# Boot in written order on VectorE and ScalarE, level 16 and u of block 1 moved to ScalarE, loads hung behind levels and updates

## The chip, the cores and the metric

The kernel runs on one core of a Trainium2 chip. The metric is the device time of one execution in microseconds (us). Profiles are of single executions; the span that a profile shows is about 1.7 us shorter than the time of the same run.

## The reference

A linear attention with per-step decay (4 batches, 8 heads, 768 tokens, head size 48), whose output, laid out as 3072 tokens by 384, goes through a dense layer:

```python
for t in range(S):
    cur = np.einsum('bhd,bhe->bhde', u[None] * kt, vt)
    y[:, :, t] = np.einsum('bhd,bhde->bhe', rt, state + cur)
    state = wt[:, :, :, None] * state + np.einsum('bhd,bhe->bhde', kt, vt)
x = y.transpose(0, 2, 1, 3).reshape(B * S, H * D)      # 3072 x 384
h = x @ w_in                                           # 384 x 2048
g = h - np.tanh(h)
return g @ w_out                                       # 2048 x 384
```

## The kernel before

The 3072 tokens are eight blocks of 384 (four batches, two halves each). For each block the attention is made in *levels*: at level m (1, 2, 4, 8, 16, 32) TensorE makes the scores between the two halves of every stretch of 2m tokens, the part that is wanted is copied into `scores`, and VectorE multiplies `kq` and `rp` by the decays of that stretch. Then come *turn* (k transposed, copied to `ks` by ScalarE), *update* (`states`, by VectorE) and *result* (two groups of matmuls, whose copies make `xT`).

```python
def level(self, ps, m, p0, n):
    if m == L // 2:                       # 32: a layout without a mask
        self.last_level(ps, p0, n)        # its copies are ScalarE's
        return self.decay(m, p0, n)
    gr = self.gram(ps, self.tiles["kq"], self.tiles["rp"], p0, n, m, L // 2)
    ins = self.decay(m, p0, n)
    ...
    for h in range(2):
        ...
        nc.vector.copy_predicated(out=dst, mask=mask, data=src)
    return ins
```

The dense layer of block i runs in 16 steps f, and the attention of block i+1 is laid between the steps. A step is: six matmuls `hp`, six results on ScalarE (`h`, `s`, `qa`, `qb`, `th`, `big`), five products on VectorE (`rest`, from `hs` to `gT`), and, three steps later, six matmuls `acc`.

Weights arrive as 64-bit words in 16 chunks of 768 KB, one for each step. Each is *converted* on the chip by two operations of ScalarE and three of VectorE:

```python
def convert(f, raw, _):
    ...
    nc.scalar.activation(out=a.bitcast(F32), in_=hi.bitcast(F32), func=AF.Copy, scale=HIGH_SCALE)
    nc.scalar.activation(out=up, in_=lo.bitcast(U32), func=AF.Copy, scale=2.0 ** -29)
    return [
        lambda: nc.vector.tensor_single_scalar(a, a, 3, op=ALU.logical_shift_left),
        lambda: nc.vector.scalar_tensor_tensor(out=a, in0=hi, scalar=-2 ** 31, in1=a,
                                               op0=ALU.bitwise_and, op1=ALU.bitwise_or),
        lambda: nc.vector.tensor_tensor(out=a, in0=a, in1=up, op=ALU.add)]
```

*Boot* is what comes before the first `hp`: the whole attention of block 0, and chunks 0 to 5. There TensorE and SyncE ran in written order, and a scheduler placed the instructions of VectorE and ScalarE. The other ten chunks are converted inside the first block, at the steps listed in `converted`:

```python
steps = (1, 2, 3, 4, 5, 6, 8, 10, 12)       # of level 1, 2, 4, 8, 16, 32, turn, update, result
before = {0: ("kmix", "rmix", "totals 1", "totals 2", "kq")}
behind = {1: ["rp"]}
converted = (0, 3, 4, 5, 5, 8, 9, 10, 11, 11)
```

`kmix` and `rmix` multiply half of k and r by u on VectorE. Last, in boot, six moves of 24 KB (`fill_holes`, `xT<-late`) copy rows that the result's layout can't put in place. The first `hp` needs them.

## Time and profile before

| | before |
|---|---|
| median, range of 4 runs | 679.27 us, 678.1 to 680.3 |
| span of the profile | 678.6 us |
| busy: TensorE, VectorE, ScalarE | 643.7, 567.3, 470.2 us |
| first `hp` begins | 49.47 us |
| VectorE begins the states of block 1 | 113.00 us |
| block 1 begins | 135.02 us |

The last rows are starts in the timeline. They cut the run into boot, the first block and the rest.

### The profile page before, as it was taken

The numbers are of one execution on the slowest core, as the hardware profiler recorded it, in microseconds if no ns is written. First come the engines' busy times: TensorE is split into PE (matmuls) and PEld (weight loads), VectorE is DVE, ScalarE is ACT, GpSimd is POOL, SyncE is SP. The second block draws the span as 40 slices with busy tenths as digits, with TensorE's granted clock in tenths as the row PEclk, the third lists the DMA queues.
The fourth block names the chain that finished last, engine by engine and source line by source line (L and its number), as shares of the span: only waits on it lengthen the run. The fifth ranks groups of instructions, "written<-read, shape, count | busy, mean of one in ns | idle before, by whom it ended". The sixth has DMA issues, their size and how long they took to land.

```text
span 678.6 us, 19964 instructions
## 1 busy us (share of the span) xinstructions
PE 643.7 (95%) x8480; PEld 412.9 (61%) x8480; DVE 567.3 (84%) x1139; ACT 470.2 (69%) x920; POOL 9.8 (1%) x30
## 2 busy tenths in 40 slices
PE   3847999999999999999999999999999999999997
PEld 3734656656665666656665666656666566655554
DVE  7899999999986998689984999769986899756764
ACT  4346779985677757686576856777576865768785
POOL 2010000000000000000000000000000000000000
PEclk9968989999999999999999999999999999999999
DMA  8788141204012321025012140124110200001000
GB/s 312 219 286 319 67 140 47 92 36 142 2 50 90 98 80 50 10 82 176 3 48 92 36 141 3 48 90 142 38 48 15 98 17 2 1 11 36 0 0 36
DMA packets 30840, 54.36 MB, mean 80 GB/s; under 512 B 2336, under 2 KB 28704, under 8 KB 30752
## 3 DMA queue, kind: packets, MB, share of 16 engines
q1 hardware_dynamic: 28960, 44.20, 19.6%
q0 software_dynamic: 1584, 8.65, 3.6%
q8 instruction: 67, 1.10, 0.7%
q10 hardware_dynamic: 208, 0.25, 0.1%
q14 instruction: 21, 0.17, 0.1%
HBM read 47.19 MB, written 4.72 MB: 76 GB/s over the span
## 4 chain that ended last, share of the span: by engine, by line
PE 78%; DVE 7%; issue 4%; PEld 4%; DMA 3%; ACT 3%; PEldq 0%; SPq 0%; DVEq 0%; ACTq 0%
PE acc L524 33%; PE hp L486 31%; PE att L238 9%; DVE states L349 2%; PE att L386 2%; PEld hp L486 2%; PE att L321 2%; PEld att L368 1%; DMA raw<-in_weights 1%; PE att L302 1%; DMA xT<-late 1%; PEld acc L524 1%; DMA wt<-in_wT 1%; DVE kq L270 1%; DVE hs L503 1%
## 5 line engine op out<-in xcount | busy, mean ns | idle before, releaser
L486 PE MATMUL hp<-xT,w_sb 128*128 128x384 f32 x768 | 273.4, 493 | 8.4 <-DMA xT<-late 6.8
L524 PE MATMUL acc<-w_sb,gT 128*128 128x384 f32 x768 | 275.0, 495 | 0.0
L486 PEld LDWEIGHTS hp<-xT,w_sb 128*128 128x128 f32 x768 | 147.6, 193 | 112.5 <-ACT up L169 7.0
L524 PEld LDWEIGHTS acc<-w_sb,gT 128*128 128x128 f32 x768 | 140.7, 190 | 89.2 <-ACT o L529 2.3
L493 ACT ACTIVATE h<-hp 128x384 f32<-128x384 f32 x128 | 62.7, 490 | 163.0 <-PE hp L486 162.4
L508 DVE TENSOR_TENSOR th<-h,th 128x384 f32<-128x384 f32 x128 | 70.9, 554 | 43.2 <-ACT th L497 43.1
L503 DVE SCALAR_TENSOR_TENSOR hs<-h,s 128x384 f32<-128x384 f32 x128 | 71.0, 555 | 23.2 <-ACT s L494 23.0
L511 DVE COPY_PREDICATED gT<-big,th 128x384 f32<-128x384 int32 x128 | 76.1, 595 | 12.8 <-ACT th L497 0.5
L495 ACT ACTIVATE qa<-s,shift 128x384 f32<-128x384 f32 x128 | 78.8, 615 | 4.2
L503 DVE SCALAR_TENSOR_TENSOR gT<-qb,hs 128x384 f32<-128x384 f32 x128 | 71.4, 558 | 9.7 <-PE hp L486 0.5
L498 ACT ACTIVATE big<-s,shift 128x384 f32<-128x384 f32 x128 | 76.8, 600 | 0.0
L496 ACT ACTIVATE qb<-s,shift 128x384 f32<-128x384 f32 x128 | 76.7, 599 | 0.0
L503 DVE SCALAR_TENSOR_TENSOR hs<-qa,hs 128x384 f32<-128x384 f32 x128 | 70.6, 551 | 0.0
L494 ACT ACTIVATE s<-h 128x384 f32<-128x384 f32 x128 | 67.0, 524 | 4.1
L238 PEld LDWEIGHTS att<-rp,kq 48*64 48x64 f32 x3072 | 54.7, 148 | 22.5 <-issue 18.9
L497 ACT ACTIVATE th<-h 128x384 f32<-128x384 f32 x128 | 64.9, 507 | 0.0
L238 PE MATMUL att<-rp,kq 48*64 48x32 f32 x3072 | 58.4, 231 | 6.1 <-issue 6.0
L270 DVE TENSOR_TENSOR kq<-kq,tot 128x768 f32<-128x768 f32 (+1 forms) x45 | 38.7, 859 | 2.6 <-PE att L238 2.6
L285 DVE COPY_PREDICATED scores<-mask_all,att 128x384 f32<-128x384 uint8 (+1 forms) x72 | 40.3, 621 | 0.0
L270 DVE TENSOR_TENSOR rp<-rp,tot 128x768 f32<-128x768 f32 (+1 forms) x45 | 38.8, 863 | 0.0
L349 DVE SCALAR_TENSOR_TENSOR states<-states,tot,att 128x48 f32<-128x48 f32 x176 | 31.5, 256 | 6.7 <-PE att L339 6.7
L238 PE MATMUL att<-rmix,kmix 48*64 48x64 f32 x768 | 14.5, 232 | 8.8 <-ACT rmix L219 6.1
(50 smaller groups left out, 338.8 us busy)
## 6 DMA issues: line engine op xcount, KB each, us to landing
raw<-in_weights POOLq DMA_DIRECT2D x11, 768.0 KB, 6.7
rmix<-in_rT SPq DMA_DIRECT2D x7, 768.0 KB, 4.7
kmix<-in_kT SPq DMA_DIRECT2D x7, 768.0 KB, 6.5
wt<-in_wT SPq DMA_DIRECT2D x7, 768.0 KB, 7.3
kq<-in_kT SPq DMA_DIRECT2D x7, 768.0 KB, 4.4
rp<-in_rT SPq DMA_DIRECT2D x7, 768.0 KB, 4.8
v_sb<-in_v SPq DMA_DIRECT2D x8, 576.0 KB, 5.7
out_y<-o SPq DMA_DIRECT2D x23, 192.0 KB, 2.0
```

Of the source, the lines that this page charges most:

```text
L238: nc.tensor.matmul(dst, lhsT=lhs[rows, t0:t0 + L], rhs=src, start=True, stop=True)
L270: ins = nc.vector.tensor_tensor(out=part, in0=part, in1=by, op=ALU.mult)
L486: nc.tensor.matmul(hp, lhsT=w_in_sb[:, f, kc, :], rhs=xT[:, kc, :], start=(kc == 0), stop=(kc == KC - 1))
L494: nc.scalar.activation(out=s, in_=h, func=AF.Square)
L495: nc.scalar.activation(out=qa, in_=s, func=AF.Square, bias=shift[:, 0:1])
L496: nc.scalar.activation(out=qb, in_=s, func=AF.Square, bias=shift[:, 1:2])
L497: nc.scalar.activation(out=th, in_=h, func=AF.Tanh)
L498: nc.scalar.activation(out=big, in_=s, func=AF.Relu, bias=shift[:, 2:3])
L503: return lambda: nc.vector.scalar_tensor_tensor(out=out, in0=in0, scalar=scalar, in1=in1, op0=op0, op1=ALU.mult)
L508: lambda: nc.vector.tensor_tensor(out=th, in0=h, in1=th, op=ALU.subtract),
L511: lambda: nc.vector.copy_predicated(out=g, mask=big.bitcast(I32), data=th)]
L524: nc.tensor.matmul(acc, lhsT=g[:, j * P:(j + 1) * P], rhs=w_out_sb[:, f, :], start=(f == 0), stop=(f == NF - 1))
```

## The change

The intent: bring the first `hp` forward, take work off VectorE where it is the full engine (boot and the first block), and remove TensorE's gaps there. The diff at its core, much shortened:

```diff
 # level 16 is copied by ScalarE, without a mask
+            if 2 * m % 32 == 0:
+                for par in range(2):
+                    for b in range(nb):
+                        ...
+                        nc.scalar.copy(out=dst[:, :, :, t0:t0 + m], in_=src[:, :, :, b, :])
+                return ins
 # the plan of the first block
-            steps = (1, 2, 3, 4, 5, 6, 8, 10, 12)
-            before = {0: ("kmix", "rmix", "totals 1", "totals 2", "kq")}
+            steps = (1, 2, 3, 4, 5, 7, 9, 10, 12)
+            before = {0: ("totals 1", "totals 2", "kq")}
-            converted = (0, 3, 4, 5, 5, 8, 9, 10, 11, 11)
+            converted = (0, 3, 4, 4, 6, 9, 9, 10, 11, 11)
 # written order in boot on all four engines
-    ctx.enter_context(tc.manual_schedule(engines={PE, SP}))
+    ctx.enter_context(tc.manual_schedule(engines={PE, SP, DVE, ACT}))
+    def boot(ps, blk, later):
 ...                                   # first half's totals early, between the two mixes
+        for m in (2, 4, 8, 16, 32):
+            for p0 in HALVES:
+                ins = blk.level(ps, m, p0, UP)
+                ...
+            begin_behind(ins, background.pop(0)())      # a load begins behind each level
+            if m <= 8:
+                ready.append(convert(*raws.pop(0)))     # ScalarE's part of chunks 0, 1, 2
+            if m in (8, 16):                            # u of block 1, by ScalarE
+                later.mix(0, NPAIR, ("rmix" if m == 8 else "kmix",), copies=False)
+        converted()                                     # VectorE's part of chunk 0
+        for p0 in HALVES:
+            blk.turn(ps, p0)
+        converted()                                     # chunk 1
+        for _ in range(2):
+            ready.append(convert(*raws.pop(0)))
+        begin_behind(blk.update(ps, h1), later.load("kq", kT, 0, NPAIR))
+        begin_behind(blk.update(ps, h2), more_weights(nc.sync))         # load of chunk 5
+        blk.result(ps, [h1, h1 + 1])
+        blk.fill_holes([nc.sync, nc.scalar, nc.sync, nc.scalar, nc.sync, nc.sync])
+        blk.result(ps, [h2, h2 + 1], True)
+        converted()                                     # chunk 2
+        more_weights(nc.sync)
+        later.load("rp", rT, 0, NPAIR)
+        more_weights(nc.sync)
+        later.load_v()
+        ready.append(convert(*raws.pop(0)))             # ScalarE's part of chunk 5
+        while ready:
+            converted()                                 # chunks 3, 4, 5
+            if ready:
+                more_weights(nc.gpsimd)
```

## The prediction

> **What bounds the kernel now.** The page first: the share of the span that each engine is busy says TensorE (95%), but that is an average over two regimes, so I went to the forty slices and then to the stretches that they suggest.
>
> ```profile
> PE   3847999999999999999999999999999999999997
> DVE  7899999999986998689984999769986899756764
> PEclk9968989999999999999999999999999999999999
> ```
>
> From the fifth slice on TensorE is full. Before that it isn't, while VectorE is, and the clock granted to TensorE dips in slices 3, 4 and 6. The same by stage: boot up to the first transposes, end of boot, the first matmuls of the first dense block, its middle, its end, and one whole later block:
>
> ```profile
> 0.00:32.00 32.00, 18.92 (x587) 17.86 (x588) 25.44 (x67) 13.19 (x25) 3.87 (x19) 1.00 0.77 264
> 32.00:49.50 17.50, 8.04 (x292) 6.66 (x290) 15.88 (x40) 8.81 (x14) 2.80 (x5) 0.72 0.87 277
> 49.50:70.50 21.00, 16.89 (x224) 10.03 (x224) 20.02 (x33) 10.57 (x20) 1.05 (x2) 0.75 0.83 300
> 70.50:97.50 27.00, 25.41 (x439) 16.20 (x440) 26.69 (x44) 22.07 (x40) 2.11 (x4) 0.94 0.27 90
> 97.50:135.00 37.50, 37.36 (x381) 23.62 (x380) 36.57 (x80) 34.87 (x65) 0.00 (x0) 1.00 0.24 79
> 135.00:213.30 78.30, 78.16 (x1070) 49.81 (x1069) 67.75 (x138) 54.73 (x110) 0.00 (x0) 1.00 0.20 65
> ```
>
> The columns after the stretch's length are busy us of PE, PEld, DVE, ACT and POOL, then granted clock, DMA share, GB/s. In the last row, which stands for 543 us of the 678.6, TensorE works 78.16 of 78.30 us: nothing that relieves VectorE or ScalarE there can show. In rows 1 to 5 VectorE is the full one (20.02 of 21.00, 26.69 of 27.00, 36.57 of 37.50). So the change can win only before 135 us, and only as much as it shortens what VectorE does there, or what holds the end of boot.
>
> That end is read in the timeline, ScalarE, SyncE and TensorE:
>
> ```profile
> 38.45 0.48 ACT L399 COPY xT<-att 128x384 f32<-128x384 f32 x1 [1.47 <-PE att L386]
> 41.25 0.92 ACT L168 ACTIVATE w_sb<-raw 128x768 f32<-128x768 f32 x1 [2.32 <-DMA raw<-in_weights]
> 42.06 0.47 ACT L399 COPY late<-att 128x384 f32<-128x384 f32 x1
> 42.56 2.49 SPq L406 DMA_DIRECT2D xT<-late  x4
> 44.11 0.90 ACT L169 ACTIVATE up<-raw 128x768 int32<-128x768 uint32 x1 [1.57 <-DVE w_sb L172]
> 44.91 1.91 ACT L399 COPY xT<-att 48x384 f32<-48x384 f32 x4
> 49.47 4.04 PE L486 MATMUL hp<-xT,w_sb 128*128 128x384 f32 x6 [6.84 <-DMA xT<-late]
> ```
>
> ScalarE stands 2.32 us before a weight chunk that has not landed, with the `late` copy ready behind it. The six small moves that fill the holes of xT leave only at 42.56 and the first dense matmul waits 6.84 us for them, where a later block has them in 1.9 us (median of the page's list of issues): three 768 KB loads are in flight beside them. The six matmuls take 4.04 us instead of 1.94, as the clock is at half.
>
> And inside the first dense block, VectorE then TensorE:
>
> ```profile
> 62.53 0.94 DVE L270 TENSOR_TENSOR rp<-rp,wt 128x768 f32<-128x768 f32 x1
> 63.58 2.79 PE L238 MATMUL att<-rp,kq 48*64 48x32 f32 x96 [2.58 <-issue]
> 88.93 1.01 PE L302 MATMUL att<-rp,kq 48*32 48x32 f32 x96 [1.55 <-DVE rp L270]
> ```
>
> The gap of 2.58 is labelled "issue", but it ends as rp is decayed (62.53 + 0.94): it too is VectorE. From the timeline's starts of hp, the first block takes 49.47 to 135.0, 85.5 us; a later one takes 78.24, and the first lacks the three acc groups carried over (3 x 1.94 = 5.8), so 72.4 would be free of loss. About 13 us are lost there, plus what boot itself could give.
>
> **What the Trainium skill says.** "TensorE: Matmul & The Clock Gate", section "HAM oscillation — how this bites in real kernels": idle of more than about 3.4 us sends the array back to half clock, and warming takes about as long. The trace agrees in kind: groups of six cost 4.04 and 4.17 us after the gaps of 6.84 and 2.58 and 1.94 otherwise; but here 2.58 sufficed. "Runtime: NRT & Kernel Launch", section "Instruction fetch mechanics": instructions come in blocks of 256 and the crossing is mostly hidden. Here TensorE stops 1.78, 1.09 and 0.50 us in boot, each after about 127 matmuls with their loads; the change alters none of that stream, so I leave these stops in. "DMA: Bandwidth & Descriptors", section "Queues, rings and completion order": engines go round the queues by packets and each ring is in order. That fits holes that land 6 us late behind bulk loads. "ScalarE: Activation LUTs", section "What ACT_TABLE_LOAD costs", gives a fixed part near 186 ns plus 0.833 ns an element; for 192 elements that estimates 346, and the trace has 310 for the copies of level 32, which I use.
>
> **The change, part by part.**
> Level 16 without a mask, boot. VectorE loses four copies in two pairs of 0.62 and 0.63: 1.25 us. The first pair lies before a wait for TensorE's level-16 matmuls (until 27.46), so decays end only about 0.55 earlier, 30.5 instead of 31.06; the rest turns to idle there. ScalarE gains 8 copies of 16 x 192, as level 32's (8 in 2.57): 2.6 us.
> u of block 1. VectorE loses two of 0.95, stride 0.87: 1.75. ScalarE gains 8 of 467 ns, stride 0.42: 3.4 us.
> ScalarE's new 6.0 us mostly lie in an idle 7.77 us (20.37 to 28.14). rmix lands at 16.16 + 4.6 = 20.8: its four are done by 22.5. Level 16 follows its matmuls: 25.3 to 26.6 and 27.5 to 28.8. kmix is there by 25.2 but stands behind: 28.8 to 30.5. Level 32 then takes 30.5 to 33.0 (before: 28.14 to 30.7), and the ks copies 33.0 to 34.6 (before: from 31.27, the second from 32.55). So the state update begins at about 35.0 instead of 33.55.
> Written order on VectorE. Two whole weight chunks (0.55 + 0.95 + 0.95, stride 2.2 each) now stand before the update: 30.5 + 4.4 = 34.9. This fills the wait for ks, so VectorE does not stand idle; before, only 1.5 chunks' first parts stood there. The update ends at 39.3 (before 37.84).
> Written order on ScalarE. No weight load stands ahead of `late`. TensorE is 1.45 later than before at that place: L386 of the first half ends about 40.2, `late` at 40.0 to 40.6, holes leave at 40.6 instead of 42.56. Loads: one chunk (begun behind the update, 39.4) is the main thing in flight, and lands by 44; holes landed by about 45.5. TensorE's second half ends near 44.4 (before 42.63), the four xT copies near 46.3 (1.91 long, no weight conversion ahead). First dense matmul: 46.5 instead of 49.47, limited by the copies, not the holes: 3.0 gained. It will still run at half clock.
> VectorE from there to the states of block 1, which before begin at 113.07. From 35.0 the old work takes 113.07 - 33.55 = 79.5 us; less what now stands before the update (2.6), less u (1.75), less level 16 in step 5 (0.94 by stride), less old waits (0.57, 0.44, 0.32, 0.25: 1.6); plus a new wait of about 1.5, as chunk 5 is converted by ScalarE only after the xT copies (46.3 + 0.9, VectorE ready at 45.9), plus 0.5 for small ones. Sum: 35.0 + 79.5 - 2.6 - 1.75 - 0.94 - 1.6 + 2.0 = 109.6, so 3.5 earlier. TensorE reached the result matmuls about 1 us after the states were ready; that slack can go too. Level 32 two steps after level 16 removes the gap of 1.55 and its half-clocked matmuls (3.35 and 2.69 instead of 1.94 each, 2.2 together), but TensorE then comes upon VectorE at w_in of step 11 (two chunks converted in step 9 now) and at the states. So 3.5 to 4.5, about 4.2, at the end of the first block.
> Later blocks: two masks of 0.52 on VectorE become four copies of about 0.47 on ScalarE (28 copies, 13 us over the run), off the path: in step 8 ScalarE has 3.1 + 1.9 = 5.0 us against TensorE's 5.6.
> Sum: 680.0 - 4.2 = 675.8.
>
> **The rivals.**
> A: ScalarE becomes the bound in boot, and the first matmul gains nothing (it moves by the 1.5 us of ks, and copies wait for chunk 5). For: my ScalarE schedule is full from 27.5 to 34.6. Against: 2.32 + 1.57 us of waits for weights go. Total then about 678.5.
> B: the removed gaps and cold stretches all come back as gain (the whole 13 us, plus 3 of boot): 664 to 668. For: levels are moved for it. Against: VectorE is 95 to 99% busy from 49.5 to 97.5 and loses only 4 us of work.
> C: loads now bunch behind the holes (two chunks, rp, v and two more from GpSimd, some 5 MB at about 300 GB/s, 17 us from 43), and rp or chunk 6 is late for steps 0 and 1. It would cost 1 to 2 us: 677 to 678. The rp decay is due near 60, so I think it holds.
> D: ScalarE's extra copies delay h in each later block: 0.5 us times 6, 678 to 679. Against: it waits 162 us for hp in the run.
>
> **Range and chances.** The mechanism gives 3.5 to 4.5; clock windows and instruction fetches may shift by a gap of about 2 us either way, rivals A, C, D take away up to 3, a part of B could add 3. Median 675.8, 672.2 to 678.6 for 8 in 10. Two per cent is 13.6 us: only B entire would reach it. Faster 0.03, same 0.96, slower 0.01.
>
> **What would show it.** The first hp matmul at 46.5 (45.5 to 47.5) and not waiting for `xT<-late`; holes leaving near 40.6 and landing in under 5 us; the ks copies from 33.0 and the states from 35.0; half clock still at the first hp; a gap of 2 to 3 us still before the level-2 matmuls of step 2 and none before level 32 in step 7; states of block 1 beginning at 109 to 110; the first block ending near 130.8; later blocks of 78.2. It is wrong if ks begins before 32 (ScalarE is faster than I think: the gain could be 6), if the holes are still awaited, or if later blocks change length at all.

## More of the kernel before

All runs told of here are in the fast state. A run of one core has no second die to compare with, so its state is judged by its time alone.

## The result, and the profile after

| | runs | median us | range us | ratio of fast runs, 95% |
|---|---|---|---|---|
| before | 4 | 679.27 | 678.1 to 680.3 | |
| after | 4 | 676.65 | 676.54 to 677.44 | 0.9964 (0.9944 to 0.9985) |

A ratio is the mean time of a kernel's fast runs over that of the fast runs of the kernel before in the same rounds, so it isn't quite the ratio of the medians. The change saves 2.6 us, 0.4%. That is less than the two per cent from which a kernel counts as faster. The prediction had 4.2, counted from 680.0: the kernel before was profiled in a run of 680.4 us, above the median, and the two profiled spans differ by 2.9.

The forty slices of the changed kernel, TensorE and the clock granted to it:

```profile
PE   3767999999999999999999999999999999999997
PEclk9988999999999999999999999999999999999999
```

Against before, the dip of the clock in the sixth slice (half clock from 90.78 to 94.19 us before) is gone and those of the third and fourth remain. By stage, in the columns that the prediction explains, from the second stretch on:

```profile
32.00:49.50 17.50, 10.82 (x297) 8.63 (x296) 16.63 (x40) 10.99 (x20) 1.21 (x2) 0.87 0.71 249
49.50:70.50 21.00, 16.14 (x310) 10.16 (x309) 20.16 (x34) 12.12 (x24) 1.05 (x2) 0.79 0.87 338
70.50:97.50 27.00, 26.76 (x357) 16.73 (x357) 26.69 (x44) 25.68 (x49) 2.11 (x4) 1.00 0.26 92
...
132.50:210.50 78.00, 77.72 (x1068) 49.61 (x1067) 67.45 (x137) 55.96 (x114) 0.00 (x0) 1.00 0.19 62
```

VectorE is as full as before (20.16 of 21.00, 26.69 of 27.00), ScalarE has taken on 3.6 us between 70.5 and 97.5 (25.68, before 22.07), and the whole later block is TensorE's as before.

The end of boot in the timeline of the changed kernel (start, duration, engine, line, operation; in brackets the idle time before it and its releaser):

```profile
31.40 0.56 DVE L170 TENSOR_SCALAR w_sb<-w_sb 128x768 int32<-128x768 int32 x1
31.99 0.96 DVE L171 SCALAR_TENSOR_TENSOR w_sb<-raw,w_sb 128x768 int32<-128x768 int32 x1
33.09 0.96 DVE L173 CUSTOM_DVE_ANT_0 w_sb<-w_sb,up 128x1536 uint16<-128x1536 uint16 x1
33.97 0.55 DVE L170 TENSOR_SCALAR w_sb<-w_sb 128x768 int32<-128x768 int32 x1
...
36.52 4.28 DVE L360 SCALAR_TENSOR_TENSOR states<-states,tot,att 128x48 f32<-128x48 f32 x24
...
40.87 0.33 SPq L159 DMA_DIRECT2D raw<-in_weights  x1
41.29 2.51 SPq L418 DMA_DIRECT2D xT<-late  x4
42.71 1.93 ACT L411 COPY xT<-att 48x384 f32<-48x384 f32 x4 [2.05 <-PE att L398]
46.92 4.18 PE L466 MATMUL hp<-xT,w_sb 128*128 128x384 f32 x6 [4.25 <-DMA xT<-late]
```

Two things are to be seen. A chunk takes VectorE 2.57 us now (31.40 to 33.97). In the kernel before, where the scheduler had alternated two chunks, it took 2.20, over the same three durations:

```profile
39.50 0.55 DVE L171 TENSOR_SCALAR w_sb<-w_sb 128x768 int32<-128x768 int32 x1
39.97 0.95 DVE L174 CUSTOM_DVE_ANT_0 w_sb<-w_sb,up 128x1536 uint16<-128x1536 uint16 x1
40.84 0.95 DVE L172 SCALAR_TENSOR_TENSOR w_sb<-raw,w_sb 128x768 int32<-128x768 int32 x1
41.70 0.55 DVE L171 TENSOR_SCALAR w_sb<-w_sb 128x768 int32<-128x768 int32 x1
```

There each operation starts 0.08 us before the recorded end of the one ahead (39.50 + 0.55 = 40.05, next at 39.97). In written order the second starts 0.03 after the end of the first (31.96, 31.99) and the third 0.14 after that of the second (32.95, 33.09), because each reads what the one just ahead wrote: 0.11 and 0.22 us lost, six chunks in boot.

The other is the first `hp`: it is at 46.92, 2.55 earlier, and still waits for the holes. SyncE issues four of them from 41.29, behind the load of chunk 5 at 40.87.

The first block, TensorE and VectorE:

```profile
61.92 2.79 PE L240 MATMUL att<-rp,kq 48*64 48x32 f32 x96 [3.34 <-issue]
...
89.83 1.01 PE L313 MATMUL att<-rp,kq 48*32 48x32 f32 x96 [0.24 <-DVE rp L272]
...
107.64 0.94 DVE L173 CUSTOM_DVE_ANT_0 w_sb<-w_sb,up 128x1536 uint16<-128x1536 uint16 x1
108.73 2.17 PE L466 MATMUL hp<-xT,w_sb 128*128 128x384 f32 x6 [1.10 <-ACT qb L476]
111.06 3.58 DVE L360 SCALAR_TENSOR_TENSOR states<-states,tot,att 128x48 f32<-128x48 f32 x20
```

The gap before level 2 stands (3.34, before 2.58), the one before level 32 is gone (0.24, before 1.55), and a new one of 1.10 has come before `hp` of step 11: it is put down to ScalarE's `qb`, but ends as VectorE finishes that step's weights (107.64 + 0.94 = 108.58). The states of block 1 begin at 111.06, 1.94 earlier. Between 30 and 115 us the record has one single wait of VectorE for another engine (us in total, times, longest), where the kernel before has five, of 2.2 us together:

```profile
DVE kq L272 <- PE att L240: 0.3, 1, 0.3
```

Block 1 begins at 132.08, 2.94 earlier. From there to the end both kernels take 543.6 us.

### The profile page after: what moved, and what is told of

Its sections match the earlier page's. It is cut to its first block, busy times and chain, and to the rows that moved or that the text cites. A ratio compares the mean times of both kernels' runs of the same rounds, so it can differ in the third digit from the quotient of the medians.

```text
span 675.7 us, 19997 instructions
## 1 busy us (share of the span) xinstructions
PE 642.5 (95%) x8480; PEld 413.0 (61%) x8480; DVE 559.9 (83%) x1119; ACT 488.1 (72%) x964; POOL 7.8 (1%) x25
## 4 chain that ended last, share of the span: by engine, by line
PE 76%; DVE 11%; issue 5%; PEld 4%; ACT 2%; DMA 2%; PEldq 0%; SPq 0%; DVEq 0%; ACTq 0%
PE acc L504 32%; PE hp L466 30%; PE att L240 9%; DVE states L360 3%; PE att L398 2%; PEld hp L466 2%; PEld att L380 1%; PE att L332 1%; DVE w_sb L171 1%; DVE hs L483 1%; DVE w_sb L173 1%; PEld acc L504 1%; DVE rp L272 1%; PE att L313 1%; DMA wt<-in_wT 1%
## 5 line engine op out<-in xcount | busy, mean ns | idle before, releaser
L491 DVE COPY_PREDICATED gT<-big,th 128x384 f32<-128x384 int32 x128 | 76.2, 595 | 12.8 <-DVE gT L483 0.5
L296 DVE COPY_PREDICATED scores<-mask_all,att 128x384 f32<-128x384 uint8 (+1 forms) x54 | 32.0, 659 | 0.0
```

What stands on the lines that cost most here:

```text
L491: lambda: nc.vector.copy_predicated(out=g, mask=big.bitcast(I32), data=th)]
```

## The experiments

Three theories of what sets the gain. **V**: VectorE's queue, from boot to the states of block 1, sets the end of the first block, and every microsecond put on it or taken off it counts. **H**: the first `hp`, with the holes and the copies of xT, sets it. **G**: TensorE's gaps and half-clocked stretches in the first block set it. Beside these the prediction's rival **C**: loads that come late.

All kernels gave correct results and were timed in five rounds against the kernel before. The changed kernel itself ran as a control. Six runs each (five for the written order alone), against 10 to 12 of the kernel before, whose median was 679.32, 679.14 and 680.01 us in the three groups of kernels that ran together (first four, next four, last four). All twelve ran on one chip. Starts in their profiles, in us:

| kernel | block 0: states begin | first `hp` | block 1: totals begin | block 1: states begin | end | end less states |
|---|---|---|---|---|---|---|
| before | 33.55 | 49.47 | 52.13 | 113.00 | 678.6 | 565.6 |
| after | 36.52 | 46.92 | 51.06 | 111.06 | 675.7 | 564.7 |
| control | 36.07 | 46.64 | 50.61 | 110.61 | 675.5 | 564.9 |
| chunks alternating | 36.31 | 47.59 | 51.53 | 111.17 | 676.4 | 565.2 |
| rp decayed in step 0 | 35.58 | 46.51 | 50.12 | 111.94 | 676.5 | 564.6 |
| chunk 5 by GpSimd | 36.03 | 45.47 | 50.46 | 110.09 | 674.5 | 564.4 |
| needless VectorE work | 35.91 | 46.73 | 50.45 | 114.69 | 679.8 | 565.1 |
| u on VectorE | 36.13 | 46.73 | 52.40 | 112.41 | 677.2 | 564.8 |
| mask for level 16 | 36.37 | 47.44 | 50.91 | 111.74 | 677.2 | 565.5 |
| old plan | 36.04 | 47.17 | 50.57 | 110.61 | 675.7 | 565.1 |
| written order alone | 35.03 | 48.20 | 62.65 | 122.90 | 687.5 | 564.6 |
| chunk 5 behind the totals | 35.63 | 47.26 | 46.80 | 112.33 | 677.7 | 565.4 |
| the same, steps alternating | 35.59 | 47.38 | 46.77 | 112.02 | 677.2 | 565.2 |
| totals by GpSimd too | 36.65 | 47.64 | | 112.39 | 677.6 | 565.2 |

("Totals" are the first work of block 1 that VectorE does in the changed kernel.) The last column says most: whatever a kernel does, its span is the start of block 1's states plus 564.4 to 565.6 us, over a range of 12.8 us of that start. So what has to be explained is when VectorE begins them.

### Control, and chunks alternating in boot

Labels `e0_after` (the changed kernel, unedited) and `e1_pairs`.

> The changed kernel itself, as the control of this group. All theories: 2 to 3.5 us below the kernel before (ratio 0.995 to 0.997), first hp matmul near 46.9, states of block 1 from 111, first block ending near 132.

Measured: 676.68 us (676.26 to 677.62), ratio 0.9959 (0.9938 to 0.9980). The result stands.

```diff
-        converted()                          # three operations of one chunk in a row
-        ...
+        (s0, o0, a0), (s1, o1, a1) = ready.pop(0), ready.pop(0)
+        ...                                  # shift, and/or, add of two chunks in turn
+        for op in (s0, s1, o0, o1, a0, a1):
+            op()
+        ...
+        for op in (s2, o2, s3, a2, o3, s4, a3): ...      # and (o4, s5, a4), (o5, a5)
```

> The six weight chunks of boot converted on VectorE with the steps of two chunks alternating, so that no step stands directly behind the one it reads. Theory V (VectorE's queue up to the states of block 1 sets the end of the first block): a chunk takes 2.2 us instead of 2.57, states of block 1 begin 1.3 to 2.0 us earlier than in the changed kernel (near 109.5), total 1.2 to 2 us below it. Rival G (gaps and half clock of TensorE are what costs): the gap before level 2 in step 2 and its clock stay, total within 0.5 us of the changed kernel. Rival H (the holes of xT, that is the first hp matmul, set the total): gain only as far as the first hp comes earlier, 0.3 to 0.7 us.

Measured: 678.50 us (677.08 to 680.13), ratio 0.9986 (0.9962 to 1.0010). Chunks did come every 2.2 us, but the time was lost again. TensorE, then VectorE, of this kernel:

```profile
44.75 0.55 PE L398 MATMUL att<-scores,v_sb 64*48 64x64 f32 x22 [2.17 <-issue]
```

```profile
48.22 0.56 DVE L170 TENSOR_SCALAR w_sb<-w_sb 128x768 int32<-128x768 int32 x1 [1.75 <-ACT w_sb L167]
```

VectorE waits 1.75 us for ScalarE's part of chunk 5, which stands behind the copies of xT, and those are late (done at 47.27, in the control 45.87) because TensorE stopped 2.17 us before its last 22 matmuls of boot. The late copies explain about half of the wait: in the control ScalarE finished that part of chunk 5 at 47.26, so VectorE, ready here at 46.47, would still have waited 0.8 (an estimate from the two traces). The stop goes with a fetch of instructions: the queue that brings TensorE's began one, of 16 KB, at 42.39 in this run and at 39.49 in the control. Twelve of the fourteen profiles have a stop at this place, of 0.1 to 2.7 us, and in each TensorE goes on 2.2 to 2.5 us after this fetch begins. In the other two (control, mask for level 16) it comes there 3.5 and 4.5 us after, and doesn't stop. What sets the start of the fetch, no run shows. So V was too simple: the wait that I had predicted for the change appears only as VectorE gets faster.

### rp of block 1 decayed in step 0

```diff
-            before = {0: ("totals 1", "totals 2", "kq")}
-            behind = {1: ["rp"]}
+            before = {0: ("totals 1", "kq", "rp"), 1: ("totals 2",)}
+            behind = {}
```

> rp of block 1 decayed in step 0 right behind kq, ahead of the first activation products; the totals from 4 up come a step later. Same VectorE work. Theory V: the gap of 3.3 us before level 2 in step 2 goes, but TensorE then waits before level 4 or later by about as much; states of block 1 within 0.5 us of 111, total within 0.7 us of the changed kernel. Rival G: total 3 to 6 us lower (3.3 us of gap and some 3 us of half clock behind it). Rival H: no change.

Measured: 678.71 us (677.90 to 684.84, five of six up to 678.84), ratio 1.0003 (0.9967 to 1.0038). VectorE and TensorE:

```profile
54.76 0.96 DVE L272 TENSOR_TENSOR rp<-rp,wt 128x768 f32<-128x768 f32 x1 [2.23 <-DMA rp<-in_rT]
```

```profile
62.27 2.63 PE L240 MATMUL att<-rp,kq 48*64 48x32 f32 x96 [2.96 <-DVE scores L247]
```

It is 2.0 us over the control, more than any theory expected. rp had not landed (2.23 us of waiting, the only wait on VectorE's record here), so rival C is real where rp is wanted before about 55 us; in the changed kernel it is used at 60.88. And the gap before level 2 stayed, released now by the masks of level 1, whose PSUM buffer it takes. The gap was not removed, so this run doesn't test G.

### The load of chunk 5 by GpSimd's queue

```diff
-        begin_behind(blk.update(ps, h2), more_weights(nc.sync))
+        begin_behind(blk.update(ps, h2), more_weights(nc.gpsimd))
```

> The load of weight chunk 5, behind the state update in boot, issued by GpSimd instead of SyncE, so that the four holes that SyncE moves don't stand behind it. Holes then leave at about 40.4 instead of 41.3 on SyncE and share the engines instead of queueing behind 768 KB. First hp matmul 1 to 2 us earlier (45 to 46). Theory V: states of block 1 and the total unchanged within 0.5 us. Rival H: total lower by what the first hp gains, 1 to 2 us. Rival G: less idle before the first hp, perhaps full clock there, 1 to 3 us lower.

Measured: 676.97 us (676.20 to 678.16), ratio 0.9962 (0.9940 to 0.9984): as the control.

```profile
39.83 3.28 SPq L418 DMA_DIRECT2D xT<-late  x4
45.47 4.27 PE L466 MATMUL hp<-xT,w_sb 128*128 128x384 f32 x6 [2.03 <-DVE w_sb L173]
```

With SyncE's queue free the holes left 1.5 us earlier than in the changed kernel, 1.0 earlier than in the control (40.83), and were no longer awaited. The first `hp` came at 45.47, as the copies of xT ended (45.42; the label names a weight conversion, but chunk 0, the one that this `hp` reads, had been converted before the states at 36.03). It is 1.17 earlier than in the control, and the time is no better. H falls for the changed kernel: the first `hp` isn't what the end waits for.

### Needless work on VectorE

```diff
+            if i == 0 and f == 6:
+                for _ in range(8):
+                    later.totals_again(2)        # 0.6 us each, result unused
```

> Eight needless VectorE operations of 128x384 (a total computed again, about 0.5 us each, 3.8 to 4.4 us in sum) in step 6 of the first dense block, where TensorE has a full queue. Theory V: states of block 1 and the total later by 3.3 to 4.4 us. Rivals G and H: TensorE has the work of other steps to go on with, 0 to 1.5 us.

Measured: 681.41 us (680.33 to 682.06), ratio 1.0025 (1.0001 to 1.0048), 4.7 us over the control. The eight operations took 4.61 us to the start of the next one, the states of block 1 came 4.08 later, the end 4.3. Work added to VectorE in the first block comes out nearly whole at the end, as V says; under H or G part of it would have been hidden.

### u of block 1 back on VectorE, and the masks of level 16 back

```diff
-            if m in (8, 16):
-                later.mix(0, NPAIR, ("rmix" if m == 8 else "kmix",), copies=False)
-            before = {0: ("totals 1", "totals 2", "kq")}
+            before = {0: ("kmix", "rmix", "totals 1", "totals 2", "kq")}
```

> u of block 1 back on VectorE (two of 0.95 us, as before), all else as changed; ScalarE loses 3.1 us in boot. Theory V: 1.3 to 1.8 us above the changed kernel. Rival H: ks and with it the first hp up to 0.7 us earlier, total the same or 0.5 lower. Rival G: within 0.5.

Measured: 679.21 us (678.91 to 681.48), ratio 0.9999 (0.9977 to 1.0022), 2.5 over the control; the states of block 1 are 1.8 later, as the two removed operations' 1.75.

```diff
-            if 2 * m % 32 == 0:
+            if False:
-    mask_cols = {1: ..., 8: slice(128, 160)}
+    mask_cols = {1: ..., 8: slice(128, 160), 16: slice(160, 192)}
```

> Level 16 masked on VectorE again in boot and in all blocks, all else as changed. Theory V: the boot part mostly fills a wait for TensorE (0.1 to 0.8 us), the part in step 5 costs 0.94: 0.9 to 1.7 us above the changed kernel; blocks from the second on of unchanged length (78.24). If ScalarE's copies in later blocks cost something, those blocks get shorter.

Measured: 679.22 us (678.82 to 679.85), ratio 0.9995 (0.9974 to 1.0016), again 2.5 over. Boot's beginning is not the same in every profile: with the same instructions the second half's level-1 matmuls began between 10.2 and 11.7 us. So I count from there. From it to the states of block 0 is 26.16 us here and 25.09 in the control (1.07 for boot's masks), and from block 1's totals to its states 60.83 and 60.00 (0.83 for step 5's). The control has the lowest figure of the six profiles with this boot (25.09 to 25.36), so boot's masks cost 0.8 to 1.07. Undisturbed later blocks take 78.24 us in both, mask or none.

Both losses of 2.5 us are above what V expected (1.3 to 1.8 and 0.9 to 1.7), and above what the states of block 1 show (1.8 and 1.1). Part of this is the choice of profiles: the control's is of one of its slower runs (677.25), these two of the faster ones (678.91, 678.97), which leaves 1.7 for each. The rest no run explains.

### The old plan of the first block

```diff
-            steps = (1, 2, 3, 4, 5, 7, 9, 10, 12)
-            converted = (0, 3, 4, 4, 6, 9, 9, 10, 11, 11)
+            steps = (1, 2, 3, 4, 5, 6, 8, 10, 12)
+            converted = (0, 3, 4, 5, 5, 8, 9, 10, 11, 11)
```

> Steps of the levels and of the weight conversions in the first dense block as before the change, all else as changed. Theory V: the same VectorE work by the states, so total within 0.8 us of the changed kernel, though the gap before level 32 (1.5 us) and its half clock come back and the wait for w_in of step 11 goes. Rival G: 2.5 to 3.5 us above the changed kernel.

Measured: 677.11 us (676.63 to 677.60), ratio 0.9963 (0.9942 to 0.9984): as the control, within 0.4 us.

```profile
86.78 1.01 PE L313 MATMUL att<-rp,kq 48*32 48x32 f32 x96 [1.55 <-DVE rp L272]
```

The gap before level 32 came back, and half clock after it (88.22 to 91.63), and the states of block 1 still began at 110.61 as in the control. The second group of result matmuls began 1.58 us later (117.64 against 116.06), but only 0.4 or less of that is seen in the time. G falls for this gap: removing it is worth next to nothing, as TensorE waits for VectorE's states anyway. For the gap before level 2 it was not tested.

### The kernel before with written order and nothing else

```diff
-    ctx.enter_context(tc.manual_schedule(engines={PE, SP}))
+    ctx.enter_context(tc.manual_schedule(engines={PE, SP, DVE, ACT}))
```

> The kernel before with one thing changed: boot in written order on VectorE and ScalarE too, so all six weight chunks are converted after the result of boot, and no load, level or u is moved. Theory V: the state update begins near 33.5 as before, but VectorE then has no chunk to fill its waits and ScalarE starts on chunk 0 only after the xT copies (near 43), so six chunks of 2.57 us lie behind it: totals of block 1 from 58 to 62 instead of 52, total 5 to 9 us above the kernel before. A theory that the order by itself brings the gain expects a time below the kernel before.

Measured: 690.42 us (689.26 to 691.72, five runs), ratio 1.0153 (1.0130 to 1.0177): 10.4 us slower, more than I had expected.

```profile
45.44 0.56 DVE L171 TENSOR_SCALAR w_sb<-w_sb 128x768 int32<-128x768 int32 x1 [6.12 <-ACT w_sb L168]
```

The old text has all conversions behind the whole attention of block 0, and the scheduler had been pulling them into its gaps. Without it VectorE idles 6.12 us here and 2.91 before the states, and block 1's totals begin at 62.65. So the written order has no worth of its own: with the old text it loses 10.4 us, and the change has to write the conversions elsewhere to avoid that.

### Taking more off VectorE's queue: three runs

If V held in both directions, a lighter queue would gain further. First, with chunks alternating, chunk 5 is converted with the weights of step 0, behind block 1's totals, so that nothing waits for it:

```diff
-        (s2, o2, a2), (s3, o3, a3), (s4, o4, a4), (s5, o5, a5) = ready
+        (s2, o2, a2), (s3, o3, a3), (s4, o4, a4), chunk5 = ready      # returned to the main loop
+            if i == 0 and f == 0:
+                (s5, o5, a5), (s6, o6, a6) = chunk5, extra
+                extra = [s5, o5, s6, a5, o6, a6]
```

> The alternating chunk steps of e1_pairs, but chunk 5 on VectorE only among the activation products of step 0, so that VectorE does not wait for ScalarE's part of it behind the xT copies (1.75 us in e1_pairs). Theory V: states of block 1 begin 1.5 to 2.2 us earlier than in the changed kernel when counted from the second level-1 group of boot (97.5 to 98.2 instead of 99.7), total 1.2 to 2.2 us below the changed kernel (674.5 to 675.5). Rival: the alternation is worth nothing and e1_pairs lost for that reason; total 676 to 678.

Measured: 678.89 us (678.25 to 679.45), ratio 0.9980 (0.9961 to 0.9998).

```profile
46.80 0.95 DVE L258 TENSOR_TENSOR tot<-wt 128x768 f32<-128x768 f32 x1
...
52.24 0.56 DVE L483 SCALAR_TENSOR_TENSOR hs<-h,s 128x384 f32<-128x384 f32 x1 [1.88 <-ACT s L474]
53.81 0.56 DVE L488 TENSOR_TENSOR th<-h,th 128x384 f32<-128x384 f32 x1 [1.01 <-ACT th L477]
```

VectorE reached block 1's totals 3.8 us before the control, and then stood 1.88 and 1.01 us before step 0's own results: `s` comes 5.0 us after the first `hp` begins (47.26; six matmuls, mostly at half clock, then `h` and `s`) and `th` 1.6 later. The sum closes. From the totals to the states of block 1 the control takes 60.0; add 1.88 + 1.01 of waiting and 2.57 of chunk 5, which now lies in this stretch: 65.5. Measured 65.53 (112.33 - 46.80).

Second, the same with every step that converts two chunks alternating them:

```diff
+            if len(extra) == 6:
+                s1, o1, a1, s2, o2, a2 = extra
+                extra = [s1, o1, s2, a1, o2, a2]
```

> As e9_c5_later, and in the steps that convert two chunks the chunk steps alternate too. Theory V: another 0.7 us less VectorE work before the states of block 1, total 0.3 to 1 us below e9_c5_later.

Measured: 679.04 us (678.55 to 681.84), ratio 0.9989 (0.9968 to 1.0010), with the same two waits (1.89, 1.01). Third, the totals of block 1 moved to GpSimd as well:

```diff
-            nc.vector.tensor_tensor(out=nxt, ...)
+            engine = nc.gpsimd if n == NPAIR and self is blocks[1] else nc.vector
+            engine.tensor_tensor(out=nxt, ...)
```

> As e10_steps_too, and the six totals of block 1 (2.6 us of VectorE) made by GpSimd, which has nothing else to do when their data lands near 30. Theory V: states of block 1 another 2.2 to 2.6 us earlier, total 1.5 to 2.6 us below e10_steps_too, the lower end where TensorE has become the later one. If GpSimd's work slows VectorE down beside it, boot's state update comes later and part of this is lost.

Measured: 680.16 us (677.92 to 684.28), ratio 1.0008 (0.9979 to 1.0038). The wait for `s` grew to 3.72 us. All three expectations fell. In these kernels a lighter VectorE only waits longer for ScalarE's results of step 0, which hang on the first `hp`.

## Why the prediction was right or wrong

The class was right, and so was the mechanism: the change wins only before the second block, by what VectorE sheds. The size was too large, 4.2 us where 2.6 came (2.9 between the profiled runs). By the steps:

**The decays and the two chunks before the update.** Predicted 34.9 to 35.0 for the states of block 0; measured 36.52. This is the step that failed, in its term "Two whole weight chunks ... stride 2.2 each" (stride: from one start to the next). They took 31.40 to 36.52, 2.56 each, as a chunk whose operations follow one another pays 0.37 more than two alternating: 0.74 of the 1.52 us. Nearly all the rest is that decays ended 0.9 later than predicted, 0.86 of it a later start of the second half's level 1 (11.18, before 10.32), which scatters as much between profiles of one boot. I had read the 2.2 off a stretch that the scheduler had alternated, and used it for an order in which nothing alternates.

**From there to the states of block 1.** Predicted 74.6 us (109.6 - 35.0), measured 74.54 (111.06 - 36.52). The sum holds, but not all its terms: the "new wait of about 1.5" for chunk 5 didn't come, since the four chunks converted in this stretch took 4 x 0.37 = 1.5 us longer and VectorE arrived that much later. It came, 1.75 long, once the chunks alternated. Nor are the copies of xT what the changed kernel would have waited for. They were done at 44.64, and ScalarE then stood 1.95 us for the load of chunk 5:

```profile
46.59 0.93 ACT L167 ACTIVATE w_sb<-raw 128x768 f32<-128x768 f32 x1 [1.95 <-DMA raw<-in_weights]
```

It was done at 47.52, and VectorE came to chunk 5 at 48.51, 0.99 later. Two errors of equal size cancelled here, and the one in the term before did not.

**u of block 1, 1.75 us** on the path: right (1.8 by undoing it). **Level 16 in step 5, 0.94**: right (0.83 to 0.87). **Level 16 in boot**, of which the prediction let "only about 0.55" count and called the rest idle: wrong, undoing it cost 0.8 to 1.07. It was too low, so it can't explain the shortfall.

**The first `hp`**, 46.5 predicted and 46.92 measured: right in time, wrong in cause. "Limited by the copies, not the holes": the copies were done at 44.64 and the holes were awaited, as they stood behind chunk 5 on SyncE. With that load elsewhere the copies do limit it. It made no difference, as it isn't the bound.

**TensorE's slack at the result**, "about 1 us": from the start of the states to the second group of result matmuls is 5.45 us now and was 6.80, so 1.35 came. **Gaps**: level 2's stayed and level 32's went, as predicted, but the second was worth no more than 0.4 us. **Later blocks** of 78.24: right for the undisturbed ones. Two of them take 78.9 and 79.5 in the changed kernel; two took 79.6 and 79.5 before. Block 1 takes 78.46, before 78.25.

**Two readings.** "In rows 1 to 5 VectorE is the full one" holds for rows 3 and 4 alone. In rows 1 and 2 it is busy 25.44 of 32.00 and 15.88 of 17.50 us, and in row 5 TensorE is the fuller one (37.36 of 37.50). And the holes didn't "land 6 us late": they took 5.9 and 6.5 us (medians of the two queues) from issue to landing, about 4 more than the 1.9 of later blocks.

**The rivals.** A (ScalarE's new work in boot takes the gain): not so in the whole; the first `hp` did gain 2.55 us. B (gaps and half clock come back as gain): refuted for level 32's by the old plan, which has that gap and no later states; level 2's gap stayed, so it could give nothing. C (late loads): from 30 us to the states of block 1 VectorE waits for none in the changed kernel, but ScalarE does for chunk 5 (1.95 us), and rp in step 0 shows how near the others are. D (later blocks): refuted, masks or copies leave the undisturbed ones at 78.24.

**What removing each part is worth**, in the states of block 1: u 1.8 and level 16 1.6 to 1.9, together 3.4 to 3.7. Counted from the second half's level 1, the control gained 3.05 (99.63 against 102.68 before) and the changed kernel 2.8. So all the rest of the change (order, loads, plan) is a net loss of about 0.4 to 0.9 on this path, by this subtraction: an estimate, which takes the parts to add up. The times of undoing each (2.5 and 2.5, against a gain of 2.6) would make it 2.4; the sign is the same, the size stays open. Its main entry against is what written order costs the six chunks (6 x 0.37 = 2.2), which the waits that it removed don't quite pay back.

**What stays open.** Two queues nearly balance in the changed kernel: VectorE's, and boot's end through the first `hp` to step 0's `th`. With `th` wanted 0.47 us after `hs` begins, and coming 6.55 after the first `hp` (53.81 - 47.26), VectorE could have begun `hs` at 46.92 + 6.1 = 53.0, where it began at 54.54: an estimate of 1.5 us of room. Taking chunk 5's load off SyncE gave the second queue 1.2 us, alternating chunks gives the first at most 2.2 (6 x 0.37), and less if chunk 5, ready only 0.99 us ahead of VectorE, comes no sooner; each alone gained nothing or lost. Both in one kernel, which is the case that could gain, was not run. No version tried beat the changed kernel; chunk 5 by GpSimd and the old plan equal it.

## What to carry to other kernels

Take a chain's cost from a stretch in which it runs in the order it will have, not from one where a scheduler put other work between its links: here the same three operations took 2.57 us in a row and 2.20 alternating. Before crediting a removed gap, find the one instruction whose start fixes the end (here the first states of block 1, plus 565 us in fourteen profiles), and credit only what moves it. And when adding work to a queue costs its whole length, don't conclude that removing it gains as much: the next wait may lie a microsecond behind.

## What the Trainium skill lacked or had wrong

- "VectorE: DVE Perf Modes", section "The DRAIN you can't avoid", measures that a semaphore after each of a chain of VectorE operations costs nothing extra. It gives no time for operations that read what the one just ahead wrote, and there the runs show a cost: in this kernel 0.11 and 0.22 us a link, 2.57 us a chunk instead of 2.20.
- "TensorE: Matmul & The Clock Gate", the section on HAM oscillation, has idle of more than about 3.4 us as what cools the array. Here half clock came with shorter ones: it was granted from 63.47 to 70.30, as a gap of 2.58 us before level 2 ended (63.58), and from 90.78 to 94.19, 1.85 us after the end of one of 1.55 before level 32. The old plan has the second pair again (1.44 us after), and the changed kernel, without that gap, has neither. Why so little suffices, no run shows.
- "Runtime: NRT & Kernel Launch", section "Instruction fetch mechanics", calls a block's crossing mostly hidden. At one place in boot it often isn't: before its last 22 matmuls there TensorE stopped for 0.1 to 2.7 us in twelve of fourteen profiles, and went on 2.2 to 2.5 us after a 16 KB fetch had begun. One stop, of 2.17 us, had a part in VectorE's wait of 1.75.
